# Row maxima turned two or three steps later, their rows written from ScalarE's queue, and one set of three PSUM banks for scores, turn and logits, in a causal attention with routed experts behind it

## The chip, the cores and the metric

One core of a Trainium2 chip. The core has TensorE (PE) for matrix products, VectorE (DVE), ScalarE (ACT), GpSimd (POOL) and SyncE (SP), which only issues transfers. Each engine works through its own list of instructions in order. Here DMA transfers are issued by SP and ACT as well as by POOL; an engine that issues one goes on as soon as the issue is done, unless the instruction itself has to wait for something. The metric is the device time of one execution in microseconds (us). Three executions of the kernel before took 743.34, 747.02 and 748.52 us, median 747.02.

## The reference

Three stages, each feeding the next:

```python
# attention: 4 batches, 8 heads, 576 positions, 64 wide
cum = np.cumsum(np.maximum(s, 0.0), axis=-1)
scores = q @ k.T / 8 + np.minimum(-(cum[i] - cum[j]), 0.0)      # only j <= i, the rest -1e9
attn = np.exp(scores - scores.max(-1)); attn /= attn.sum(-1) + 1e-9
x = attn @ v                                                    # laid out as batch, position, 512
# routed experts: 8 experts, 512 -> 1024 -> 512
logits = x @ w_gate; local = sigmoid(x @ w_local)
e[s] = argmax(logits[s]) if s == 0 or local[s] < 0.5 else e[s-1]
y[s] = softmax(logits[s])[e] * (relu(x[s] @ w1[e]) @ w2[e])
# gated unit: 512 -> 1024 -> 512, a convolution of width 3 along the positions
h = relu(y @ w_in)
out = (h * sigmoid(conv3(h, conv_w))) @ w_out
```

All products have to come out near single precision, so operands are split into a high and a low half-precision part, and a product becomes two or three matrix products.

## The kernel before, in words

**Stages.** Attention runs until about 263 us, then the last logits, the choice of experts and the sorting of tokens (a chain on DVE with short matrix products), then the experts' matrix products from 299 us on, then the gated unit. The change touches only attention and the logits that are made beside it.

**Units and steps.** Attention is cut into eight units, one for four heads of one batch. A unit is 14 steps: for each head the score groups g = 0, 1, 2 and, behind each pair of heads, g = 3 (the last 64 positions of both). `scores` at step t multiplies k by q on PE into a tile z (pool `zps`, three banks of PSUM, L438 and L441). One step later `weights` makes two exponentials of it on ACT, phi in half precision (L475) and p in single (L476). Two steps later `rest` makes the low part plo on DVE (L487). At step 4 behind a pair's last group PE multiplies by v (`values`, L503); normalising and writing out (`norm`, `xout`, `store`, `put`) follow.

**The row maxima.** The exponential needs the maximum of each row of scores, as one more row of k: row 70 of the tiles `K1`, and of `T1` for the tails. It comes from a first, coarser product that is made for a coming unit beside the current one: `stage_a` gives 14 pieces, each some matrix products into a tile za (pool `aps`, two banks, L331) and a reduction on DVE (`mx`, L334). Behind the last piece stand four steps: `max_cols` (DVE, tile m, L397), `max_turn` (PE, one product with the identity that turns the 128x18 columns of maxima into 18 rows, L407, in pool `mps`, one bank), `max_out` (ACT copies the 18 rows into the tile mr, L412) and `max_row` (three transfers: two of eight rows into `K1`, L419, and one of two rows into `T1`, L422). The first `scores` of the unit needs the first of them, and the third `scores` of the unit, at its index 2, the last.

**What sets the order.** Every engine's list is written in program order by a loop over steps t. Work that is not tied to t itself is planned by the table `PAR`: a number says how many steps ahead of a unit's first step t0 the thing is done. `mx` is the step of `max_cols`: -3 for unit 1, -6 for unit 2, -5 for unit 3 and -7 for the units 4 to 7. `max_turn` and `max_out` stand one step behind it, `max_row` two. `at` sets splitting, transposing (`turn`, L256) and copying (L260, L264) of a unit's k and q, `load` and `lv` the loads (L160, L170), `ps` the step at which a finished unit's result is written to memory (`put`, L573, L577). All these transfers are issued by SP (`Q`), in program order; ACT issues only three small ones at the start (L590, L591).

**What a transfer waits for.** Besides the data it needs, each transfer issued by SP or ACT raises one of eight completion counters (DMAHW0 to DMAHW7), which are handed out in turn when the program is built, in the order in which the builder expects the transfers. Before it is issued, its engine waits until the transfer that used that counter last has landed. An engine waiting so does nothing else.

Of the kernel before, what the change touches and what calls it, by code (L numbers as in the profile page):

```python
# [9 lines left out]
F32 = mybir.dt.float32  # L10
# [6 lines left out]
PSUM = bass.MemoryType.PSUM  # L17
# [25 lines left out]
class Keep:  # L43
# [3 lines left out]

PAR = {'u1': {'sv': -6, 'pa': -10, 'pn': 4, 'mx': -3},  # L50
 'u2': {'at': (-24, -23, -20, -20, -19, -16), 'lv': -15, 'sv': -2, 'pa': -14, 'pn': 8, 'mx': -6},
 'u3': {'load': -37, 'loadq': 6, 'at': (-33, -28, -28, -27, -24, -22), 'sv': -1, 'pa': -19, 'pn': 14, 'mx': -5},
 'u': {'load': -48,
       'loadq': 8,
       'at': (-38, -34, -28, -31, -23, -23),
# [1 line left out]
       'sv': -4,  # L57
       'pa': -20,
       'pn': 13,
       'mx': -7},  # L60
 'h': {'rc': 11,
       'lg': 16,
       'co': 1,
# [51 lines left out]
def attention(tc, ctx, q, k, v, s, xd, rt, hook):  # L115
# [8 lines left out]
    V, A, PE, Q, G = nc.vector, nc.scalar, nc.tensor, nc.sync, nc.gpsimd  # L124

    def pool(n, b, on=ctx, **kw):
        return on.enter_context(tc.tile_pool(name=n, bufs=b, **kw))

    const, vp, natv = pool("const", 1), pool("vv", 2), pool("natv", 1)
    pp, p0p, php, wk, xp, xtp = pool("p32", 3), pool("p0", PAR["h"]["p0"]), pool("phl", PAR["h"]["ph"]), pool("wk", 2), pool("xs", 2), pool("xt", 1)  # L130
    zps, aps, ops, mps = (pool(n, b, space=PSUM) for n, b in (("zps", 3), ("aps", 2), ("ops", 2), ("mps", 1)))
    dram = pool("exd", 1, space=bass.MemoryType.DRAM)
    ex, ext = dram.tile([3, 2, B * H, 256], F16, name="ex"), dram.tile([3, B * H, 64], F16, name="ext")
    *big, st2 = hook(-1)
# [16 lines left out]
    T1, T2 = const.tile([71, B, 2, 512], F16, name="t1"), const.tile([128, B, 2, 512], F16, name="t2")  # L151
    U = {}
    src, scale, AT = dict(q=q, k=k), dict(q=QS, k=KS), dict(k=0, q=1)

    def load(u, n):
        b, h0 = u // (H // NH), u % (H // NH) * NH
        t = big[n == "q"][:, 0:1024] if u % 2 == 0 else big[1][:, 1024 + 1024 * AT[n]:2048 + 1024 * AT[n]]
        t = U[u, n] = t.rearrange("p (h c d) -> p h c d", h=NH, c=2)
        for c in range(2):
            Q.dma_start(t[:, :, c], src[n][b, h0:h0 + NH, 256 * c:256 * c + 256].rearrange("h (p t) d -> p h (t d)", t=2))  # L160
# [42 lines left out]
    for tq, tk, n in ((triq, trik, 64), (tailq, tailk, 32)):  # L203
        for r in range(0, 128, n):
            x = dict(compare_op=ALU.is_ge, fill=-2.0 ** 15)
            t, r = r // n % 2, slice(r, r + n)
# [42 lines left out]
    def split_qk(u, n):  # L249
        split_hi(u, n)  # L250
        split_lo(u, n)
# [14 lines left out]
    def split_tail(n):  # L266
        i = AT[n]
        a, h = nt[:, i].rearrange("p h (t d) -> p (h t) d", t=2), ht[:, i]
        A.activation(h[:, :, 1 - i], a, AF.Copy, scale=scale[n])
        V.scalar_tensor_tensor(h[:, :, i], in0=a, scalar=scale[n], in1=h[:, :, 1 - i], op0=ALU.mult, op1=ALU.subtract)  # L270
# [11 lines left out]
    def split_v(u):  # L282
# [10 lines left out]
        for x, dh, dl in ((a, w[:, :, :, 0, 0:64], w[:, :, :, 1, 0:64]), (t, wt[:, :, 0, 0:64], wt[:, :, 1, 0:64])):  # L293
            if u == 0 or not PAR["h"]["vg"]:
                A.activation(dh, x, AF.Copy, scale=VS)
# [89 lines left out]
    def key(hs):  # L385
        return hs.start if hs else 16

    def span(hs, tails):
        return slice(0 if hs else 16, 18 if tails else 8)
# [12 lines left out]
            V.tensor_scalar(m[:, 16:18], mx[:, 16:18], 2.0 ** -12, None, op0=ALU.mult)  # L402

    def max_turn(u, hs=slice(0, 4), tails=True):
        t = U[u, "mt"] = mps.tile([128, 512], F32, name="mt")
        r = span(hs, tails)
        PE.matmul(t[0:r.stop - r.start, 0:128], lhsT=U[u, "16", key(hs)][:, 0:r.stop - r.start] if key(hs) != 16 else U[u, "16", 16][:, 16:18], rhs=id16, start=True, stop=True, skip_group_check=True)  # L407

    def max_out(u, hs=slice(0, 4), tails=True):
        n = span(hs, tails).stop - span(hs, tails).start  # L410
        mr = U[u, "mr", key(hs)] = wk.tile([18, 128], F16, name="mr")
        A.activation(mr[0:n], U[u, "mt"][0:n, 0:128], AF.Copy)  # L412

    def max_row(u, hs=slice(0, 4), tails=True):
        n = 0
        if hs:
            n = 4 * (hs.stop - hs.start)
            for e in range(2):
                Q.dma_start(U[u, 1][70:71, e, 1, 256 * hs.start:256 * hs.stop].rearrange("o (x c) -> o x c", c=128), U[u, "mr", key(hs)][n // 2 * e:n // 2 * e + n // 2])  # L419
        if tails:  # L420
            c = 256 * (u % 2)
            Q.dma_start(T1[70:71, u // 2, 1, c:c + 256].rearrange("o (r c) -> o r c", r=2), U[u, "mr", key(hs)][n:n + 2])  # L422

    st = {}

    def mode(x):

        return PAR["m"][3 * x[1] + x[2]] if x[2] < 3 else "a"

# [121 lines left out]
    def store(u, part):  # L551
# [3 lines left out]
        xh, eng = U[u, "xh"][:, part], G if u < NU - 1 else V  # L555
        if eng is G and PAR["h"]["xg"]:
            G.tensor_copy(xh[:, :, 0], x)
# [41 lines left out]
    def plan(t, f):  # L599
        todo.setdefault(math.floor(t), []).append((t, len(todo), f))  # L600
# [14 lines left out]
    def second_a():  # L615
# [5 lines left out]
        lk1=lambda: load(1, "k"), lq1=lambda: load(1, "q"), st=lambda: (split_tail("k"), split_tail("q")), tt=turn_tail, ct=copy_tail,  # L621
        lv0=lambda: loadv(0, 0, G), lv1=lambda: loadv(0, 1, G if PAR["h"]["vq"] else Q), c1=lambda: constants(G, K1[1]), c2=lambda: (constants(G, K1[2]), tctx.close()),
        pa=begin_a, sk1=lambda: split_qk(1, "k"), sq1=lambda: split_qk(1, "q"), mt0a=lambda: max_turn(0, first, False), mo0a=lambda: max_out(0, first, False),
# [4 lines left out]
        z=lambda: Q.dma_start(xd[NT:NT + 128].rearrange("p (j c) -> p j c", c=256), bc(zero[:, None], [128, 4, 256])))  # L628
    for n, t in PAR["start"].items():
        plan(t, begin_tasks[n])  # L630
# [8 lines left out]
    for u in range(1, NU):  # L639
        t0 = u * PER  # L640
        c = PAR.get(f"u{u}", {}) if u < 4 else PAR.get("u", {})
        if u > 1:
            if u > 2:
                plan(t0 + c["load"], lambda u=u: load(u, "k"))
                plan(t0 + c["load"] + c["loadq"], lambda u=u: load(u, "q"))
            for x, f in zip(c["at"], (lambda u=u: split_qk(u, "k"), lambda u=u: split_qk(u, "q"), lambda u=u: turn(u, 0), lambda u=u: turn(u, 1),
                                 lambda u=u: (extra(u), copy(u, "k")), lambda u=u: copy(u, "q"))):
                plan(t0 + x, f)
        if u % 2 == 0:
            plan(t0 + c["lv"], lambda u=u: loadv(u // 2))  # L650
        plan(t0 + c["sv"], lambda u=u: split_v(u))
        for i in range(14):
            pieces.setdefault(t0 + c["pa"] + i * c["pn"] // 14, []).append((u, i))
        plan(t0 + c["mx"], lambda u=u: max_cols(u))
        plan(t0 + c["mx"] + 1, lambda u=u: max_turn(u))
        plan(t0 + c["mx"] + 1, lambda u=u: max_out(u))
        plan(t0 + c["mx"] + 2, lambda u=u: max_row(u))
    for t in sorted(x for x in todo if x < 0):
        work(t)
    am, P = [], {}  # L660
    for t in range(N + 9):
        if t == N - 2 * PER - 6:
            early.close()
        for f in am:
            f()
        am = []
        work(t)
        at = lambda d: steps[t - d] if 0 <= t - d < N else None
        if at(0):
            scores(at(0))  # L670
        for u, i in pieces.get(t, ()):
            if i == 0:
                P[u] = stage_a(u)
            am.append(P[u][i]())
        if at(1):
            weights(at(1))
        if at(2):
            rest(at(2))
        for d, f in ((4, values), (5, norm), (6, xout)):
            y = at(d)  # L680
            if y and y[2] == (3 if y[1] % 2 else 2):
                f(y[0], y[1])
        y = at(7)
        if y and y[2] == 3 and y != (NU - 1, 1, 3):
            store(y[0], y[1] // 2)
        y = at(8)
        if y and y[1:] == (3, 3):
            u = y[0]
            rt.turn(u, U[u, "xh"], U[u // 2, "xth"] if u % 2 else None, range(2) if u < NU - 1 else range(1, 2))
            if u == NU - 1:  # L690
                put(u, range(1, 2))
        y = at(PAR["h"]["ps"])
        if y and y[1:] == (3, 3) and y[0] < NU - 1:
            put(y[0], range(2))
        if at(9) == (NU - 1, 1, 3):
            store(NU - 1, 0)
            rt.turn(NU - 1, U[NU - 1, "xh"], None, range(1))
            put(NU - 1, range(1))
        y = at(PAR['h']['lg'])
        if y and y[1:] == (3, 3) and y[0] < NU - 1:  # L700
            rt.logits(y[0], mps.tile([128, 512], F32, name="mt"))
        y = at(PAR['h']['lg'] + PAR['h']['co'])
        if y and y[1:] == (3, 3) and y[0] < NU - 1:
            rt.collect(y[0])
        hook(t)
# [751 lines left out]
```

## Time and profile before

| | |
|---|---|
| three runs | 743.34, 747.02, 748.52 us (median 747.02) |
| profiled execution | 745.7 us, span 743.5 us |
| busy share of the span | PE 85%, DVE 62%, ACT 52%, POOL 36% |
| chain that ended last | PE 49%, DMA 6%, DVE 1% of the span; it can be followed back to 310.5 us |
| attention | about 28 to 263 us |
| routing | 264 to 299 us |
| experts | 299 to 545 us |
| gated unit | 550 to 740 us |

The profiled execution is 1.3 us below the median of the three runs and inside their range. A row of a list of work in order of time reads: start, busy time, engine (an ending q means that the engine's sequencer issues a transfer), line, operation, tiles, and in brackets the idle time of the engine before it with what ended it. Neighbouring instructions of one kind are one row, marked x2, x3 and so on.

### The profile page before, as it was taken

The page shows a single profiled execution, that of the slowest core. Times are in us where ns is not written, and L with a number is a line of the kernel's source. Part 1 is how long each engine was busy: PE and PEld are TensorE (multiplying, and loading weights), DVE is VectorE, ACT ScalarE, POOL GpSimd, SP SyncE. Part 2 cuts the span into 40 slices and gives each one's busy share as a digit, 9 for nine tenths or more (in the row PEclk, how much of TensorE's full clock was granted, in tenths as well). Part 3 has the DMA queues.
Part 4 walks back from the last instruction along what each step waited for, and adds up shares of the span by engine and source line. Part 5 has one row for each costly group of instructions (what it writes and reads, how often), then busy time and mean ns, then how long its engine had stood idle before and what let it go on. Part 6 is the DMA issues. An engine that isn't in the chain of part 4 may idle for free.

```text
span 743.5 us, 15702 instructions
## 1 busy us (share of the span) xinstructions
PE 631.6 (85%) x5301; PEld 387.1 (52%) x5301; DVE 464.3 (62%) x838; ACT 383.3 (52%) x640; POOL 265.3 (36%) x367
## 2 busy tenths in 40 slices
PE   0449669988988934779999999999879999999997
PEld 0226547766766832334444444444347776666443
DVE  5527558987979787962587759675108994465000
ACT  4135647666767875543464737352109975455110
POOL 9316757655645247922243443433200000000000
PEclk9999879888989975998999999999989999999999
DMA  9977697878768895399999999966256400000111
GB/s 182 200 138 140 158 165 145 136 165 180 128 142 220 248 265 191 86 220 300 237 281 316 240 295 186 255 146 135 68 97 112 65 1 29 29 15 28 58 43 56
DMA packets 197278, 113.37 MB, mean 152 GB/s; under 512 B 147286, under 2 KB 173182, under 8 KB 197182
## 3 DMA queue, kind: packets, MB, share of 16 engines
q1 hardware_dynamic: 192574, 99.14, 58.5%
q0 software_dynamic: 4272, 12.93, 6.1%
q8 instruction: 48, 0.79, 0.4%
q14 instruction: 48, 0.39, 0.2%
q10 hardware_dynamic: 336, 0.11, 0.1%
HBM read 62.20 MB, written 15.31 MB: 104 GB/s over the span
## 4 chain that ended last, share of the span: by engine, by line
PE 49%; DMA 6%; DVE 1%; issue 0%; ACT 0%; another core or an unknown queue 0%; ACTq 0%; SPq 0%; DVEq 0%
PE hp L1270 13%; PE o L1318 13%; PE hp L1078 12%; PE yp L1078 11%; DMA yd<-ys,idx 4%; DMA ht<-hs 2%; PE xp L1108 1%; DVE r L1034 1%; DMA yt<-yd 0%; DVE hs L1124 0%; ACT xt L1109 0%; DVE ys L1138 0%; ACT ys L1137 0%; ACT s L1321 0%
## 5 line engine op out<-in xcount | busy, mean ns | idle before, releaser
L1078 PE MATMUL hp<-r,xt 128*128 x504 | 114.9, 385 | 8.4 <-ACT xt L1109 5.9
L1078 PE MATMUL yp<-r,ht 128*128 x504 | 112.2, 379 | 1.7 <-PEq L1186 1.1
L1270 PE MATMUL hp<-yt,wi 128*128 128x288 f16 x768 | 97.1, 289 | 2.9 <-DMA yt<-yd 2.9
L334 DVE TENSOR_REDUCE mx<-za 128x1 f32<-128x512 f32 (+4 forms) x113 | 67.7, 612 | 50.1 <-PE za L331 49.6
L1318 PE MATMUL o<-wo,g 128*128 128x512 f16 x432 | 94.5, 379 | 0.0
L487 DVE TENSOR_TENSOR plo<-p,phi 128x512 f16<-128x512 f32 (+1 forms) x104 | 85.1, 819 | 6.4 <-ACT p L476 6.2
L1270 PEld LDWEIGHTS <-wi 128*128 128x128 f16 x768 | 75.8, 99 | 24.5 <-DMA yt<-yd 3.4
L1078 PEld LDWEIGHTS <-xt 128*128 128x128 f16 x504 | 49.9, 99 | 69.5 <-ACT xt L1109 9.1
L475 ACT ACTIVATE phi<-z,lnes 128x512 f16<-128x512 f32 (+1 forms) x104 | 65.5, 629 | 39.3 <-PE z L441 39.2
L1078 PEld LDWEIGHTS <-ht 128*128 128x128 f16 x504 | 48.5, 98 | 57.4 <-issue 1.8
L331 PE MATMUL za<-k 70*128 70x256 f16 (+2 forms) x160 | 40.4, 338 | 41.3 <-DMA k<-k 33.6
L1034 DVE SCALAR_TENSOR_TENSOR r<-st,r 128x512 f32 (+3 forms) x76 | 69.3, 980 | 8.1 <-ACT r L1023 4.7
L438 PE MATMUL z<-k 71*128 71x256 f16 (+2 forms) x320 | 60.5, 311 | 12.3 <-ACT phi L475 6.7
L1139 POOL DMA_INDIRECT yd<-ys,idx x21 | 21.6, 1028 | 135.6 <-DVEq L1062 84.3
L1318 PEld LDWEIGHTS <-g 128*128 128x128 f16 x432 | 42.3, 98 | 49.5
L476 ACT ACTIVATE p<-z,lnes 128x512 f32<-128x512 f32 (+1 forms) x104 | 65.6, 631 | 1.2 <-DVE plo L487 1.1
L1023 ACT ACTIVATE r<-st 128x512 f32 (+3 forms) x84 | 57.0, 760 | 15.4 <-SPq L1071 12.5
L503 PEld LDWEIGHTS <-phi 128*128 128x128 f16 (+2 forms) x896 | 53.4, 108 | 4.8 <-issue 1.0
L503 PE MATMUL o<-vv,phi 128*128 128x65 f16 (+1 forms) x832 | 54.3, 203 | 0.0
L438 PEld LDWEIGHTS <-k 71*128 71x128 f16 x576 | 39.7, 106 | 22.7 <-issue 10.9
L503 PE MATMUL o<-vv,plo 128*128 128x65 f16 (+1 forms) x416 | 51.2, 200 | 0.0
L1287 DVE SCALAR_TENSOR_TENSOR c<-hb,cw,c 128x576 f32<-128x576 f32 x32 | 26.1, 816 | 36.7 <-ACT c L1281 36.7
(255 smaller groups left out, 1018.6 us busy)
## 6 DMA issues: line engine op xcount, KB each, us to landing
st<-in_moe_w_dram SPq DMA_DIRECT2D x8, 2048.0 KB
st<-in_moe_w_dram SPq DMA_DIRECT2D x24, 512.0 KB
out_dram<-s SPq DMA_DIRECT2D x18, 256.0 KB
st<-in_k_dram SPq DMA_DIRECT2D x16, 256.0 KB
st<-in_q_dram SPq DMA_DIRECT2D x16, 256.0 KB
k<-k SPq DMA_DIRECT2D x16, 256.0 KB
xd<-xh SPq DMA_DIRECT2D x16, 256.0 KB
k<-in_moe_w_dram SPq DMA_DIRECT2D x8, 512.0 KB
```

Source lines behind the costliest of these rows:

```text
L331: PE.matmul(out, lhsT=l, rhs=r, start=start, stop=stop, skip_group_check=True)
L334: return lambda: V.tensor_reduce(out, z.rearrange("p (e c) -> p e c", e=m), axis=AX.X, op=ALU.max)
L438: PE.matmul(out, lhsT=ks[i], rhs=qs[i], start=first and not i, stop=False, skip_group_check=True)
L475: A.activation(hi[:, 0:n], z[:, 0:n], AF.Exp, bias=lnes, scale=1.0 / SC)
L476: A.activation(p[:, 0:n], z[:, 0:n], AF.Exp, bias=lnes, scale=1.0 / SC)
L487: (V if md == "a" else G).tensor_tensor(lo[:, 0:n], p[:, 0:n], hi[:, 0:n], op=ALU.subtract)
L503: PE.matmul(out, lhsT=w, rhs=x, start=first, stop=last, skip_group_check=True)
L1023: i = self.nc.scalar.activation(hi, src, AF.Copy, scale=self.scale[w])
L1034: i = nc.vector.scalar_tensor_tensor(lo, in0=src, scalar=sc, in1=hi, op0=ALU.mult, op1=ALU.subtract)
L1078: i = self.nc.tensor.matmul(out, lhsT=lhsT, rhs=self.rings[w][:, c, k, bass.ds(s, 1), f], **kw)
L1270: PE.matmul(st[x][:, n, 0:HN], lhsT=wi[:, c, k, m], rhs=t[:, n, a + k], start=k + a + c == 0, stop=k == 3 and a == 4)
L1318: PE.matmul(o, lhsT=g[:, a, k, 128 * i:128 * i + 128], rhs=wo[:, c, k], start=j == 0, stop=j == 23)
```

## The change

The table gets an entry `mt`, the number of steps from `max_cols` to `max_turn`: 1 for unit 1, 2 for the units 2 and 3, 3 for the units 4 to 7. `max_out` and `max_row` now stand together, one step behind `max_turn` (in the same step for unit 1), and `max_row` is issued by ACT (`A`) instead of SP, but for unit 0. The pool `mps` is gone: the turn and the logits take their bank from `aps`, which has three.

```diff
-PAR = {'u1': {'sv': -6, 'pa': -10, 'pn': 4, 'mx': -3},
- 'u2': {... 'pa': -14, 'pn': 8, 'mx': -6},
- 'u3': {... 'pa': -19, 'pn': 14, 'mx': -5},
+PAR = {'u1': {'sv': -6, 'pa': -10, 'pn': 4, 'mx': -3, 'mt': 1},
+ 'u2': {... 'pa': -14, 'pn': 8, 'mx': -6, 'mt': 2},
+ 'u3': {... 'pa': -19, 'pn': 14, 'mx': -5, 'mt': 2},
  'u': {...
-       'mx': -7},
+       'mx': -7,
+       'mt': 3},
...
-    zps, aps, ops, mps = (pool(n, b, space=PSUM) for n, b in (("zps", 3), ("aps", 2), ("ops", 2), ("mps", 1)))
+    zps, aps, ops = (pool(n, b, space=PSUM) for n, b in (("zps", 3), ("aps", 3), ("ops", 2)))
...
-        t = U[u, "mt"] = mps.tile([128, 512], F32, name="mt")
+        t = U[u, "mt"] = aps.tile([128, 512], F32, name="za")
...
-    def max_row(u, hs=slice(0, 4), tails=True):
+    def max_row(u, hs=slice(0, 4), tails=True, on=Q):
...
-                Q.dma_start(U[u, 1][70:71, e, 1, ...
+                on.dma_start(U[u, 1][70:71, e, 1, ...
...
-            Q.dma_start(T1[70:71, u // 2, 1, c:c + 256]...
+            on.dma_start(T1[70:71, u // 2, 1, c:c + 256]...
...
-        plan(t0 + c["mx"] + 1, lambda u=u: max_turn(u))
-        plan(t0 + c["mx"] + 1, lambda u=u: max_out(u))
-        plan(t0 + c["mx"] + 2, lambda u=u: max_row(u))
+        plan(t0 + c["mx"] + c["mt"], lambda u=u: max_turn(u))
+        plan(t0 + c["mx"] + c["mt"] + (u > 1), lambda u=u: (max_out(u), max_row(u, on=A)))
...
-            rt.logits(y[0], mps.tile([128, 512], F32, name="mt"))
+            rt.logits(y[0], aps.tile([128, 512], F32, name="za"))
```

From line 61 to about line 654 the changed file's numbers are one higher. Three places of the lists show what moves.

The first is PE at the turn of unit 5's maxima, in the steps of unit 4 (L407 is the turn, L438 and L441 the scores of unit 4, L331 a piece of unit 6's maxima). Before it stands ahead of the second score group of the third head:

```order
L438 LDWEIGHTS k_1392
L438 MATMUL z<-k_1392 128x512
L441 LDWEIGHTS identm
L441 MATMUL z<-trik,identm 128x128
L407 LDWEIGHTS m_2926
L407 MATMUL mt<-id_134,m_2926 18x128
L438 LDWEIGHTS k_142
L438 MATMUL z<-k_142 128x128
```

In the changed kernel it stands two steps further on, behind a piece of unit 6's and ahead of the first score group of the fourth head:

```order
L442 LDWEIGHTS identm
L442 MATMUL z<-trik,identm 128x128
L332 LDWEIGHTS k_138
L332 MATMUL za<-k_138 128x256
L332 LDWEIGHTS k_138
L332 MATMUL za<-k_138 128x256
L332 LDWEIGHTS identm
L332 MATMUL za<-triq,identm 128x128
L332 LDWEIGHTS identm
L332 MATMUL za<-triq,identm 128x128
L408 LDWEIGHTS m_2923
L408 MATMUL za<-id_131,m_2923 18x128
```

So two more steps of scores and pieces stand between the making of the maxima and their turn.

The second is ACT at the same unit, with the semaphores that each row waits for. Before, its list has only the copy there, and its transfers are SP's:

```order
L475 ACTIVATE phi<-z,lnes 128x64
L476 ACTIVATE p<-z,lnes 128x64
L412 ACTIVATE mr<-mt 18x128
L238 ACTIVATE st_114<-st_115 128x16x64
L471 ACTIVATE p_2978<-z,lnes 128x512
L475 ACTIVATE phi<-z,lnes 128x512
```

Now the copy and the three transfers stand behind two more pairs of exponentials, and ahead of the pair of unit 4's index 10:

```order
L477 ACTIVATE p<-z,lnes 128x512 [waits DVE_49]
L413 ACTIVATE mr<-za 18x128 [waits DMAHW7_49,PE_49]
L420 DMA k_140<-mr 1x8x128 [waits DMAHW1_49,Activation_49]
L420 DMA k_140<-mr 1x8x128 [waits DMAHW4_49]
L423 DMA t_141<-mr 1x2x128 [waits DMAHW0_49]
L476 ACTIVATE phi<-z,lnes 128x512 [waits PE_49]
L477 ACTIVATE p<-z,lnes 128x512 [waits DVE_49]
```

The transfer of `T1`'s rows now waits on ACT for counter 0.

The third is SP in that stretch: the transposes of unit 3's result (L824, L827), those of unit 7's q (L256), and unit 3's `put` (L573). Before:

```order
L824 DMA_TRANSPOSE xT<-xh 128x16x128 [waits DMAHW4_49,Pool_49]
L827 DMA_TRANSPOSE xTt<-xth 128x4x128 [waits DMAHW5_49,Pool_49]
L419 DMA k_143<-mr 1x8x128 [waits DMAHW6_49,Activation_49]
L419 DMA k_143<-mr 1x8x128 [waits DMAHW7_49]
L422 DMA t_144<-mr 1x2x128 [waits DMAHW0_49]
L256 DMA_TRANSPOSE k_3101<-st_114 128x32x64 [waits PE_49,DMAHW1_49,Activation_49,Pool_49]
L256 DMA_TRANSPOSE k_3101<-st_114 128x32x64 [waits DMAHW2_49]
L573 DMA xd<-xh 128x4x256 [waits DMAHW3_49]
```

Changed:

```order
L824 DMA_TRANSPOSE xT<-xh 128x16x128 [waits DMAHW4_49,Pool_49]
L827 DMA_TRANSPOSE xTt<-xth 128x4x128 [waits DMAHW5_49,Pool_49]
L257 DMA_TRANSPOSE k_3098<-st_111 128x32x64 [waits PE_49,DMAHW6_49,Activation_49,Pool_49]
L257 DMA_TRANSPOSE k_3098<-st_111 128x32x64 [waits DMAHW7_49]
L574 DMA xd<-xh 128x4x256 [waits DMAHW0_49]
L574 DMA xd<-xh 128x4x256 [waits DMAHW2_49]
```

The three rows are gone from SP, and counter 0 is now used by the first half of unit 3's `put`, just ahead of the transfer on ACT that waits for counter 0 (the value it waits for is that `put`'s).

## Rows read from the trace of the kernel before

**Rows 1.** Busy time by engine in two stretches; TensorE's granted clock, DMA share, GB/s.

```profile
core 0: us, PE busy (x) PEld busy (x) DVE busy (x) ACT busy (x) POOL busy (x), PEclk, DMA share, GB/s
...
130.00:159.00 29.00, 24.35 (x362) 19.23 (x360) 26.94 (x63) 17.77 (x34) 17.16 (x20) 0.82 0.79 147
...
187.00:211.00 24.00, 20.88 (x360) 17.13 (x359) 23.62 (x58) 17.37 (x33) 13.46 (x21) 0.98 0.70 129
```

**Rows 2.** PE in order of time: its waits around the maxima, and the experts' start.

```profile
107.76 0.59 PE L331 MATMUL za<-k 70*128 70x128 f16 x4 [5.22 <-DMA k<-k]
...
154.47 0.25 PE L331 MATMUL za<-t 70*64 70x64 f16 x4 [1.82 <-DVE mx L334]
...
158.04 0.28 PE L407 MATMUL mt<-id,m 128*18 128x128 f16 x1 [1.16 <-DVE m L397]
...
171.60 0.61 PE L438 MATMUL z<-k 71*128 71x512 f16 x2 [2.30 <-DMA k<-mr]
...
186.54 0.22 PE L407 MATMUL mt<-id,m 128*18 128x128 f16 x1 [1.85 <-DVE m L397]
...
193.79 0.26 PE L438 MATMUL z<-t 71*64 71x64 f16 x4
...
210.14 0.28 PE L407 MATMUL mt<-id,m 128*18 128x128 f16 x1 [1.74 <-DVE m L397]
...
236.16 0.22 PE L407 MATMUL mt<-id,m 128*18 128x128 f16 x1 [2.05 <-DVE m L397]
...
298.84 5.34 PE L1078 MATMUL hp<-r,xt 128*128 x24 [1.26 <-ACT xt L1109]
```

**Rows 3.** DVE in order of time, behind the turns of units 4 and 6.

```profile
160.38 1.33 DVE L334 TENSOR_REDUCE mx<-za 128x4 f32<-128x512 f32 x2 [1.00 <-PE za L331]
...
213.11 1.33 DVE L334 TENSOR_REDUCE mx<-za 128x4 f32<-128x512 f32 x2 [1.63 <-PE za L331]
```

**Rows 4.** SP in order of time: transfers issued late.

```profile
8.56 8.24 SPq L256 DMA_TRANSPOSE k<-h  x4
...
102.18 1.39 SPq L264 DMA_DIRECT2D k<-k  x2
...
138.17 8.04 SPq L256 DMA_TRANSPOSE k<-st  x2
...
167.96 1.51 SPq L419 DMA_DIRECT2D k<-mr  x2
...
192.29 7.10 SPq L256 DMA_TRANSPOSE k<-st  x2
199.44 1.84 SPq L573 DMA_DIRECT2D xd<-xh  x2
```

**Rows 5.** ACT in order of time: its own transfers, unit 4's copy, unit 5's, idle places.

```profile
13.89 0.46 ACTq L591 DMA_DIRECT2D ext<-cp  x1
...
158.35 0.27 ACT L412 ACTIVATE mr<-mt 18x128 f16<-18x128 f32 x1 [1.93 <-PE mt L407]
...
166.30 0.69 ACT L475 ACTIVATE phi<-z,lnes 128x512 f16<-128x512 f32 x1 [1.90 <-PE z L441]
...
186.80 0.27 ACT L412 ACTIVATE mr<-mt 18x128 f16<-18x128 f32 x1 [1.69 <-PE mt L407]
...
190.77 0.66 ACT L475 ACTIVATE phi<-z,lnes 128x512 f16<-128x512 f32 x1
...
242.62 0.69 ACT L475 ACTIVATE phi<-z,lnes 128x512 f16<-128x512 f32 x1 [1.95 <-PE z L441]
```

**Rows 6.** POOL in order of time: the low part of unit 7's q.

```profile
189.23 2.12 POOL L247 TENSOR_TENSOR st<-st,st 128x1024 f16<-128x1024 f32 x1
```

**Rows 7.** Single lines: number, duration in ns (least, median, most), first and last start.

```profile
L419 SPq DMA_DIRECT2D k<-mr x18: 585/692/994, 34.2 to 240.2; - x18
...
L422 SPq DMA_DIRECT2D t<-mr x8: 589/598/619, 48.9 to 240.9; - x8
...
L256 SPq DMA_TRANSPOSE k<-st x8: 3075/3770/4744, 38.8 to 195.4; - x8
```

More of the change, by code (lines that the diff above doesn't have):

```diff
@@ L44 @@
     pass
-PAR = {'u1': {'sv': -6, 'pa': -10, 'pn': 4, 'mx': -3},
- 'u2': {'at': (-24, -23, -20, -20, -19, -16), 'lv': -15, 'sv': -2, 'pa': -14, 'pn': 8, 'mx': -6},
- 'u3': {'load': -37, 'loadq': 6, 'at': (-33, -28, -28, -27, -24, -22), 'sv': -1, 'pa': -19, 'pn': 14, 'mx': -5},
+PAR = {'u1': {'sv': -6, 'pa': -10, 'pn': 4, 'mx': -3, 'mt': 1},
+ 'u2': {'at': (-24, -23, -20, -20, -19, -16), 'lv': -15, 'sv': -2, 'pa': -14, 'pn': 8, 'mx': -6, 'mt': 2},
+ 'u3': {'load': -37, 'loadq': 6, 'at': (-33, -28, -28, -27, -24, -22), 'sv': -1, 'pa': -19, 'pn': 14, 'mx': -5, 'mt': 2},
  'u': {'load': -48,
@@ L418, in max_row @@
             for e in range(2):
-                Q.dma_start(U[u, 1][70:71, e, 1, 256 * hs.start:256 * hs.stop].rearrange("o (x c) -> o x c", c=128), U[u, "mr", key(hs)][n // 2 * e:n // 2 * e + n // 2])
+                on.dma_start(U[u, 1][70:71, e, 1, 256 * hs.start:256 * hs.stop].rearrange("o (x c) -> o x c", c=128), U[u, "mr", key(hs)][n // 2 * e:n // 2 * e + n // 2])
         if tails:
             c = 256 * (u % 2)
-            Q.dma_start(T1[70:71, u // 2, 1, c:c + 256].rearrange("o (r c) -> o r c", r=2), U[u, "mr", key(hs)][n:n + 2])
+            on.dma_start(T1[70:71, u // 2, 1, c:c + 256].rearrange("o (r c) -> o r c", r=2), U[u, "mr", key(hs)][n:n + 2])
     st = {}
```

## The prediction, as made before the changed kernel ran

> **What bounds the kernel now.** I read the chain of waits first. It can be followed back only to 310.5 us, where it lies in the experts' products, but these begin at 298.84 behind the routing [rows 2], and the routing is one serial chain of short DVE and PE instructions that begins with the last unit's result. So I take a microsecond won or lost in attention as a microsecond at the end, one for one. Next I looked at attention's stretches by engine. In 130 to 159 us DVE is busy 26.94 of 29 us and PE 24.35; in 187 to 211 us DVE 23.62 of 24 and PE 20.88; ACT has 17.77 of 29 and 17.37 of 24 [rows 1]. DVE is the tight engine there, and ACT has about a third of its time free. Then I read PE's list for its waits [rows 2]: 5.22 us for a copy of k, 1.82 for a maximum on DVE, 2.30 for the maxima rows of unit 4, and 1.16, 1.85, 1.74 and 2.05 at the turns of units 4 to 7, where PE stands until `max_cols` is done. Last I read SP's list, because the 2.30 is no matter of data: unit 4's rows lay ready at 158.62 (the copy's 158.35 + 0.27 [rows 5]), and SP issued them at 167.96 [rows 4], 9.3 us later, because other transfers stood ahead.
>
> The sum is made against the profiled execution, 745.7 us; the median of the runs, 747.02, is 1.3 above it.
>
> **Gains, place by place.**
>
> The turns of units 4 to 7 come two steps later (a step is about 2 us: 14 of them lie in some 28 us). All four waits are under 2.1 us, so they go whole at their place; the question is what they hide. Behind the turns of units 4 and 6 DVE sits idle for 1.00 and 1.63 us, waiting for the piece that PE makes next [rows 3]: there the wait of PE became a wait of the tight engine. I take the two waits whole, 1.2 and 1.7 (bounds 0 and that). Behind the turn of unit 5 DVE has no hole; it is busy in all but 0.4 us of the 24 [rows 1], so PE catches up and waits for DVE instead: 0 (at most 1.85). At unit 7 PE has little of its own to wait for otherwise, and ACT shows a hole of 1.95 behind [rows 5]; I take half of the 2.05: 1.0 (0 to 2.05).
>
> Unit 4's rows on ACT: the copy is issued two pairs of exponentials later than now, at about 163, three issues behind it take under 2 us (0.692, 0.692 and 0.598 on SP [rows 7]), and landing takes 2.1 (issue ended 167.96 + 1.51 = 169.47, PE freed at 171.60 [rows 2, 4]). That is 167, ahead of the 169.3 at which PE came. The 2.30 goes (0 to 2.3); next late there would be DVE's reductions.
>
> SP gets 2.0 us shorter per unit (the same three issues). Its list is without holes where the copy of k for the 5.22 us wait is issued at 102.18 [rows 4], and unit 1's rows stand ahead of it, so that copy comes up to 2.0 earlier: 2.0 (0 to 2.0).
>
> The third bank for za lets PE run one piece further ahead of DVE. It can only save where PE waits for a reduction, as in the 1.82 at 154.47; DVE stays the bound there: 0.5 (0 to 1.8). While a turn or logits hold one of the three banks, two are left, which is what za has now, so I set no loss against it.
>
> The gains are 1.2 + 1.7 + 0 + 1.0 + 2.3 + 2.0 + 0.5 = 8.7; all upper ends together make 12.9.
>
> **Losses.**
>
> ACT's own work: three issues for each of seven units. On ACT an issue took 0.46 once, on SP 0.59 to 0.99 [rows 5, 7], so 1.4 to 2.0 per unit, 10 to 14 in all. ACT waits for z for 1.90 and 1.95 us at such places [rows 5] and has a third of its time free, so a pair of exponentials that comes 1.5 later still comes before PE runs out of banks for z (three). I take 0.5 (0 to 4, two units uncovered).
>
> The counters. Here a new wait is added to ACT, and behind it on ACT stand all later exponentials. **At unit 5** the transfer of `T1`'s rows waits for counter 0, which unit 3's `put` used last. That `put` stands on SP behind the two transposes of unit 7's q, and these need POOL's low part, which ends at 191.35 (189.23 + 2.12 [rows 6]). Before, they were issued from 192.29 for 7.10 us and the `put` followed at 199.44 [rows 4]. With SP's own three rows gone they can begin at 191.4 at the earliest, or at 189.7 if ACT's share of the split is not held by the 1.69 us wait for the turn any more [rows 5]; the first half of the `put` is then issued by 197.7 to 199.4 and lands 2.1 later, at 199.8 to 201.5. ACT comes to the waiting transfer where unit 4's pair of index 10 begins now, 190.77 [rows 5], plus about 1 for the two issues ahead. So ACT stands for 8 to 9.5 us. PE can make the z of two or three more steps and has the values of older steps to do; it stops about at index 13, 193.79 [rows 2], until the pair of index 10 is done, about 201. Once freed, ACT catches up at 0.66 per exponential [rows 5]. DVE, the bound, has about 2 us of reductions and subtractions in hand, then waits as well. I price it at what DVE loses, 8 minus 2, so 6; bounds 3 (if half is made up behind) and 9 (nothing in hand). It does not lock up: nothing that the `put` needs stands behind that transfer.
>
> **At unit 3** the same transfer waits for one of SP's transposes for unit 5, issued before from 138.17 for 8.04 both [rows 4]; only the first counts, and it can begin about 2 earlier without SP's rows. ACT would come at about 139.5: hold 0 to 2.5, taken as 0.5, as DVE's list behind covers most. At unit 7 a margin of about half a microsecond is left, at units 1, 2, 4 and 6 the counters' earlier transfers are old: 0.
>
> The losses are 0.5 + 6 + 0.5 = 7.0.
>
> **Sum.** 745.7 - 8.7 + 7.0 = 744.0, and 745.3 when set beside the median: I forecast 745, no change that can be told from none. One per cent is 7.5 us here, about what a measurement of this kernel can tell.
>
> **A rule against the change.** SP's four transposes at the start were in issue from 8.56 to 16.80 [rows 4], and inside that time ACT issued a transfer in 0.46 us at 13.89 [rows 5]: no sign that the one holds up the other. The Trainium skill, "Perfetto Trace Analysis", section "DMA Instruction — HWDGE (DVE, Sync)", says that the block which makes the descriptors is locked for one instruction's exclusive use, and that the next sequencer's lock wait counts in the shown duration; by that, ACT's rows would each wait for a transpose's issue. The row speaks against it, but the rule makes a rival.
>
> **The rivals.**
>
> *No hold (0.25).* If unit 3's `put` lands before ACT comes, or PE, DVE and ACT have more in hand than I think, the 6 does not come. For it: ACT may come later than 191, since the whole of attention moves. Against it: 7.10 us of transposes stand ahead of the `put`. The time: 745.3 - 6 = 739; with the upper ends of two turns and the banks, 736.
>
> *ACT's issue is held by SP's transposes (0.08, slower).* At units 2 to 7 SP has transposes beside the rows; one takes 3.77 us at the median [rows 7]. ACT has about 1.9 free at such a place, so each would cost 1.9, six of them 11: 745.3 + 11 = 756. It decides if ACT's issues take over 1.5 us each. Against it: 0.46 at 13.89.
>
> *A longer hold (0.09, slower).* ACT's wait at unit 5 delays its share of what POOL and SP need next, so that the units behind it find their `put` and transposes late too, unit 7 first, whose margin is half a microsecond. With the hold at 9, unit 3's at 2.5 and a third of 3, and the gains at half (4.3), the time is 747.0 - 4.3 + 14.5 = 757. It decides if ACT's wait at unit 5 is over 10 us or comes at a second unit with over 2.
>
> *My forecast (0.58)*, gains and hold nearly cancel: 740 to 751, by the bounds 3 and 9 of the hold and some 5 up or down in the gains.
>
> **The numbers.** Faster by over 1% (under 739.5) is three quarters of the first rival and a tenth of the forecast: 0.25. Slower by over 1% (over 754.5) is nearly all of the two slow rivals and a tenth of the forecast's upper side: 0.18. The rest, 0.57, is within 1%. The range leaves out the far part of the first rival and of the two slow ones: 737 to 753.
>
> **What would show it.** Right: no wait at the turns of units 4 to 7; no wait for mr's rows at unit 5's beginning (171.60 now); on ACT at about 191 to 200 an idle stretch of 8 us or so in front of L423, ended by `xd<-xh`, with PE waiting behind for ACT's phi and DVE for p; ACT's issues of about 0.5 us each. Wrong: no such stretch (then the first rival), issues of 2 us and more on ACT (then the second), a second hold at units 3 or 7 (then the third), or the PE waits at the turns coming back as waits for DVE's mx in the pieces beside them, in which case the gains were never there and the time is 750.

## The result and the profile after

Four of five executions of the changed kernel took 752.85 to 755.6 us; the median of all five is 754.1. The ratio to the kernel before is 1.0105 (95% interval 1.0063 to 1.0147). It is 1% slower; 745, no change, was forecast, and the range ended at 753. The fifth execution took 1698.08 us, more than twice the others, and is left out of the ratio. The kernel before was run five times in all; its median stays 747.02. The profiled execution took 754.1 us with a span of 751.5, which is 8.0 more than before.

The loss lies in attention: the experts' first product starts at 308.59 where it started at 298.84 [rows 2], 9.75 later. PE's list of the changed kernel in order of time, at the places of [rows 2]:

```profile
104.68 0.58 PE L332 MATMUL za<-k 70*128 70x128 f16 x4 [2.48 <-DMA k<-k]
...
144.17 1.01 PE L439 MATMUL z<-k 71*128 71x512 f16 x2 [4.26 <-DMA k<-mr]
...
164.28 0.27 PE L408 MATMUL za<-id,m 128*18 128x128 f16 x1 [3.64 <-DVE mx L335]
...
188.01 0.58 PE L332 MATMUL za<-k 70*128 70x128 f16 x4 [3.52 <-DVE plo L488]
...
202.65 0.32 PE L439 MATMUL z<-t 71*64 71x64 f16 x4 [5.48 <-ACT p L477]
...
225.49 0.22 PE L408 MATMUL za<-id,m 128*18 128x128 f16 x1 [1.71 <-DVE mx L335]
...
245.05 0.22 PE L408 MATMUL za<-id,m 128*18 128x128 f16 x1 [0.89 <-DVE m L398]
...
308.59 0.59 PE L1078 MATMUL hp<-r,xt 128*128 x2 [1.26 <-ACT xt L1109]
```

The wait for k has gone from 5.22 to 2.48, and that for unit 4's rows is gone. The waits at the turns are gone at unit 5 only: at unit 7 0.89 is left, and at units 4 and 6 they are 3.64 and 1.71, now ended by a reduction of a piece (`mx`, L335) instead of `max_cols`. Three waits are new: 4.26 for unit 3's rows, 3.52 for `plo` at 188.01, and 5.48 for p at 202.65. Behind the last stands ACT, here at unit 5's rows, in order of time:

```profile
191.81 0.25 ACT L413 ACTIVATE mr<-za 18x128 f16<-18x128 f32 x1
192.09 2.27 ACTq L420 DMA_DIRECT2D k<-mr  x2
200.70 0.59 ACTq L423 DMA_DIRECT2D t<-mr  x1
201.34 0.69 ACT L476 ACTIVATE phi<-z,lnes 128x512 f16<-128x512 f32 x1 [9.27 <-DMA xd<-xh]
```

SP beside it:

```profile
190.16 6.21 SPq L257 DMA_TRANSPOSE k<-st  x2
196.41 2.82 SPq L574 DMA_DIRECT2D xd<-xh  x2
```

ACT issues the two `K1` rows by 194.36 and then does nothing until 200.70, which is 6.3 us; the 9.27 counts from the copy `mr` to the next exponential, with the three issues in it. The profile names unit 3's `put` (`xd<-xh`), which SP could issue only at 196.41, behind its two transposes. DVE has nothing to subtract meanwhile:

```profile
202.63 0.69 DVE L488 TENSOR_TENSOR plo<-p,phi 128x512 f16<-128x512 f32 x1 [5.63 <-ACT p L477]
```

### The profile page after: what moved, and what is told of

It reads as the page before. It is cut to its first block, busy times and chain, and to the rows that moved or that the text cites. A ratio compares the mean times of both kernels' runs of the same rounds, so it can differ in the third digit from the quotient of the medians.

```text
span 751.5 us, 15698 instructions
## 1 busy us (share of the span) xinstructions
PE 634.9 (84%) x5301; PEld 393.1 (52%) x5301; DVE 466.9 (62%) x838; ACT 383.2 (51%) x640; POOL 264.2 (35%) x367
## 5 line engine op out<-in xcount | busy, mean ns | idle before, releaser
L1078 PE MATMUL hp<-r,xt 128*128 x504 | 112.2, 379 | 9.4 <-ACT xt L1109 7.9
L488 DVE TENSOR_TENSOR plo<-p,phi 128x512 f16<-128x512 f32 (+1 forms) x104 | 86.9, 837 | 15.9 <-ACT p L477 15.8
L335 DVE TENSOR_REDUCE mx<-za 128x1 f32<-128x512 f32 (+4 forms) x113 | 66.5, 612 | 40.6 <-PE za L332 40.5
L439 PE MATMUL z<-k 71*128 71x256 f16 (+2 forms) x320 | 62.2, 318 | 10.9 <-DMA k<-mr 8.1
L504 PEld LDWEIGHTS <-phi 128*128 128x128 f16 (+2 forms) x896 | 57.7, 114 | 5.4 <-issue 1.3
L504 PE MATMUL o<-vv,phi 128*128 128x65 f16 (+1 forms) x832 | 58.2, 209 | 0.0
L504 PE MATMUL o<-vv,plo 128*128 128x65 f16 (+1 forms) x416 | 54.4, 206 | 0.0
```

The source lines that it names most:

```text
L335: return lambda: V.tensor_reduce(out, z.rearrange("p (e c) -> p e c", e=m), axis=AX.X, op=ALU.max)
L439: PE.matmul(out, lhsT=ks[i], rhs=qs[i], start=first and not i, stop=False, skip_group_check=True)
L488: (V if md == "a" else G).tensor_tensor(lo[:, 0:n], p[:, 0:n], hi[:, 0:n], op=ALU.subtract)
L504: PE.matmul(out, lhsT=w, rhs=x, start=first, stop=last, skip_group_check=True)
L1078: i = self.nc.tensor.matmul(out, lhsT=lhsT, rhs=self.rings[w][:, c, k, bass.ds(s, 1), f], **kw)
```

## The experiments

The theory is that this wait of ACT, in front of all later exponentials, is what makes the change slower. The first rival: the time goes with the late turn and the shared banks, and the wait only covers it. Each ratio is to the kernel before on the same chip, with its 95% interval.

**Unit 5's `T1` row by SP.** One transfer of the change is undone.

```diff
-            on.dma_start(T1[70:71, ...
+            (Q if u == 5 else on).dma_start(T1[70:71, ...
```

> The changed kernel, but unit 5's transfer of T1's rows is issued by SP again; its two K1 rows stay on ACT and now wait for counters of transfers that landed long before (a put at 180 us, a copy from ex at 181). If the counter's wait on ACT (9.27 us in front of the exponential at 201.34) is what made the change slower: that stretch vanishes, the fifth unit begins about 8 us earlier, 746 us. If the later turn and the shared banks cost the time and the stretch only covers them: 752 to 754.

0.9991 (0.9953 to 1.0029). ACT at the same place:

```profile
190.68 0.25 ACT L413 ACTIVATE mr<-za 18x128 f16<-18x128 f32 x1
190.96 1.31 ACTq L420 DMA_DIRECT2D k<-mr  x2
192.32 0.69 ACT L476 ACTIVATE phi<-z,lnes 128x512 f16<-128x512 f32 x1 [1.39 <-PE za L332]
```

The stretch is gone, and with it the whole loss.

**Every `put` two steps later.** No row of maxima is moved; the counters fall otherwise, and the writes of the results come later.

```diff
-       'ps': 18},
+       'ps': 20},
```

> The changed kernel with every unit's put two steps later (20 in place of 18), so that the counters fall otherwise: unit 5's three transfers on ACT wait for copies of k and a transpose that landed before 185 us. Same theory as for unit 5's row on SP, without moving a row: if the counter is the cause, 746 us and no stretch on ACT at 192; if rows on ACT in themselves hold ACT, 753.

0.9971 (0.9927 to 1.0016). Three rows by ACT, no wait for a counter:

```profile
186.88 1.31 ACTq L420 DMA_DIRECT2D k<-mr  x2
188.24 0.59 ACTq L423 DMA_DIRECT2D t<-mr  x1
188.88 0.69 ACT L476 ACTIVATE phi<-z,lnes 128x512 f16<-128x512 f32 x1 [2.02 <-DMA k<-mr]
```

The 2.02 is now only the three issues and what lies between them.

**Unit 3's turn one step earlier.**

```diff
- 'u3': {... 'mx': -5, 'mt': 2},
+ 'u3': {... 'mx': -5, 'mt': 1},
```

> The changed kernel with unit 3's turn one step behind its maxima instead of two. PE waits 4.26 us for unit 3's rows at 144.17 although ACT issued them by 138.07. If they are late because they are issued late (two steps behind their old place): that wait falls to under 2.5 and the time by 2 to 3, 751 us. If they are late because transposes of SP fill the transfer engines from 132 to 140: they land at the same time and nothing changes, 754.

1.0152 (1.0102 to 1.0202). PE's wait at unit 3's start is gone, and PE waits 1.35 at that unit's turn instead. But PE now comes to that start later than the rows were there in the changed kernel, 144.17:

```profile
145.26 1.04 PE L439 MATMUL z<-k 71*128 71x512 f16 x2
```

So this run does not tell whether the rows had been late because they were issued late or because they took long to land (issued by 138.07, there at 144.17). The time did not fall. ACT still stood 8.75 us at unit 5.

**Banks as before.** Two for za, one for turn and logits, all else as changed.

```diff
-    zps, aps, ops = (... ("zps", 3), ("aps", 3), ("ops", 2)))
+    zps, aps, ops, mps = (... ("zps", 3), ("aps", 2), ("ops", 2), ("mps", 1)))
```

> The changed kernel with the banks as before (two for za, one for turn and logits); turn and queue as in the changed kernel, and the same counter for unit 5's last row. If the turn waits at 164.28 (3.64 us, ended by a reduction of za) and 225.49 (1.71) because it needs a bank that a piece still holds: both waits vanish and the time falls by 2 to 4, 751. If DVE's backlog sets the pace with either set of banks, the waits move to the pieces and the time stays at 754.

1.0203 (1.0151 to 1.0254). The wait beside unit 4's turn is still there, 3.97, now at the piece ahead of the turn:

```profile
168.20 0.59 PE L332 MATMUL za<-k 70*128 70x256 f16 x2 [3.97 <-DVE mx L335]
```

So a bank of its own for the turn does not take the wait away: it goes over to the piece, which waits for DVE's reductions too. ACT stood at unit 3 for a transpose's counter and at unit 5 for the `put`'s, longer than in the first profile of the changed kernel:

```profile
146.02 0.69 ACT L476 ACTIVATE phi<-z,lnes 128x512 f16<-128x512 f32 x1 [7.82 <-DMA k<-st]
...
206.70 0.69 ACT L476 ACTIVATE phi<-z,lnes 128x512 f16<-128x512 f32 x1 [10.29 <-DMA xd<-xh]
```

Since the waits differ too, this run says nothing on what the banks are worth.

**One part at a time.** The next four put parts of the change into the kernel before. Queue alone (turn and rows at their old places):

```diff
-        plan(t0 + c["mx"] + 2, lambda u=u: max_row(u))
+        plan(t0 + c["mx"] + 2, lambda u=u: max_row(u, on=A))
```

> The kernel before with one part of the change: the maxima rows of units 1 to 7 are issued by ACT, at their old place; turn and banks as before. Their counters were last used by transfers that should have landed (unit 5: a put issued at about 179 us in the kernel before). If SP's shorter list and unit 4's rows are the gain I priced (2.0 + 2.3): no wait for mr's rows at unit 4's start, the experts' first product 4 us earlier, 738 against 742.3 on this chip. If issuing on ACT costs as much as it saves: 742 or more, with ACT standing on counters at units 3 or 7.

0.992 (0.9883 to 0.9956), the lowest ratio of all, though some intervals below overlap it. The experts' first product starts at 292.86, 5.98 ahead of the kernel before. Unit 4 starts without a wait; PE still waits at every turn:

```profile
157.98 0.28 PE L408 MATMUL mt<-id,m 128*18 128x128 f16 x1 [1.42 <-DVE m L398]
...
169.21 0.60 PE L439 MATMUL z<-k 71*128 71x512 f16 x2
...
183.98 0.23 PE L408 MATMUL mt<-id,m 128*18 128x128 f16 x1 [2.17 <-DVE m L398]
...
207.57 0.23 PE L408 MATMUL mt<-id,m 128*18 128x128 f16 x1 [1.74 <-DVE m L398]
...
230.40 0.22 PE L408 MATMUL mt<-id,m 128*18 128x128 f16 x1 [2.06 <-DVE m L398]
```

Turn alone (`mt` as in the change, rows by SP, banks as before):

```diff
+        plan(t0 + c["mx"] + c["mt"], lambda u=u: max_turn(u))
+        plan(t0 + c["mx"] + c["mt"] + (u > 1), lambda u=u: (max_out(u), max_row(u, on=Q)))
```

> The kernel before with the later turn alone; rows by SP, banks as before. My sum's term for the turns (1.2 + 1.7 + 1.0) would give 738, less what later rows cost on SP's full list (unit 4's wait of 2.30 grows by up to 4): 738 to 742. The rival: DVE's reductions set the pace there, the waits at the turns only move to the pieces beside them, and the later rows cost 4: 746.

1.0029 (1.0001 to 1.0056), as the rival expected. PE's waits at the turns of units 4 to 6 are gone, and these stand in their place:

```profile
190.14 0.58 PE L332 MATMUL za<-k 70*128 70x128 f16 x4 [5.91 <-DMA k<-k]
...
216.47 0.38 PE L332 MATMUL za<-k 70*128 70x128 f16 x4 [2.39 <-DMA k<-k]
...
228.97 0.63 PE L439 MATMUL z<-k 71*128 71x512 f16 x2 [3.61 <-DMA k<-mr]
```

SP waits for the later `mr`, and all behind it with it: unit 7's transposes begin at 196.46, before at 192.29 [rows 4].

```profile
194.22 1.48 SPq L420 DMA_DIRECT2D k<-mr  x2
195.74 0.60 SPq L423 DMA_DIRECT2D t<-mr  x1
196.46 7.31 SPq L257 DMA_TRANSPOSE k<-st  x2
```

In this one profile the experts begin at 307.52, 8.68 later than before, while the ratio of the runs is worth only some 2 us; why the two differ is open.

Banks alone (pool `aps` with three, `mps` gone):

> The kernel before with the three shared banks alone. By my sum 0.5 faster: 742. By the comparison of the split banks in the changed kernel (1.0203 against 1.0105) sharing is worth some 7 us when turn and rows come late; if it is worth that by itself: 736 to 738.

1.0007 (0.9973 to 1.0041): nothing. The 1.82 of [rows 2] ahead of unit 4's turn is gone, and the wait at the turn has grown from 1.16 to 3.36:

```profile
157.60 0.22 PE L408 MATMUL za<-id,m 128*18 128x128 f16 x1 [3.36 <-DVE m L398]
```

With one more bank PE gets further ahead and then waits longer for the same engine.

Turn and banks, rows by SP (the changed kernel with `on=Q`):

> The changed kernel with the rows issued by SP again, turn late and banks shared. If the queue is the whole of the loss (the counter on ACT): faster than the kernel before by the turns and banks, 738 to 740. If rows that come two steps later are too late on SP's list: PE waits for mr's rows at the starts of units 3 to 6 for 2 to 6 us each, 748 or more, and the change of queue is needed with the later turn.

1.002 (0.9988 to 1.0051). PE waits for rows at the starts of units 1 and 6 (7.96 and 3.10) and for copies of k at 108.46, 158.59 and 188.10 (7.08, 3.81, 5.66); neither half of the expectation was right, the late rows cost about as much as the turns gave.

**Queue and banks, turn at its old place.**

> The changed kernel with the turn, the copy and the rows at their old places: queue and banks of the change without its later turn. If the later turn is what brings the put's counter onto ACT: no stretch of 8 us on ACT at unit 5, and the time of the queue alone, 0.992 of before. If rows on ACT and shared banks hurt each other by themselves (a turn that needs a bank of za and holds it until ACT comes): 1.00 or more.

0.9957 (0.9919 to 0.9996), an interval that overlaps the queue alone's. At unit 5 ACT has no wait for a counter: between the rows and the next exponential lie 0.79 us. The late turn is what brought them together with the `put`.

**Late turn by ACT without the wait, banks as before** (`ps` 20).

> Rows on ACT and the later turn with the banks as before, and put at 20, so that unit 5 waits for no late counter (unit 3's last row still waits for the counter of a transpose for unit 5). If the later turn is worth something once the wait for the put is gone: 0.990 or less. If it only moves PE's waits to the pieces, because DVE sets the pace: 0.992 to 1.000, and a wait of 2 to 6 at unit 3's start.

0.9958 (0.9916 to 0.9999): an interval that overlaps the queue alone's, and not the 0.990 at which the turn would have shown a worth of its own.

**One step only.** `mt` 1 for units 1 to 3 and 2 for the rest, copy and rows in the turn's step, `ps` 20.

> A version to beat both: rows on ACT together with the copy, the turn one step later for units 4 to 7 only, shared banks, put at 20; all of unit 5's counters last used by copies and a transpose that landed before. If one step is enough to take PE's waits at the turns (1.2 to 2.1 each) and they count: 0.985. If DVE sets the pace: the same as the queue alone, 0.992.

1.0006 (0.9959 to 1.0053). Neither half of the expectation was right: it is not 0.985, and it lies above the queue alone's whole interval. Why is open.

**The changed kernel again.**

> The changed kernel once more, for what a second profiled execution repeats. Attention: the experts' first product within 1.5 us of the first profile's 308.6, ACT's stretch at unit 5 of 8 to 10 us again. The experts: if the waits of 2 to 3 us with a lower granted clock behind them belong to single executions, they stand in other places or are gone, and the experts take 3 to 6 us more or less; if they belong to the kernel, they stand at 340 and 462 again. Ratio to before 1.006 to 1.015.

1.0188 (1.0125 to 1.0252). The ratio, the start of the experts' first product (311.20) and ACT's stretch are all above what was expected; ACT stood at unit 3 also:

```profile
143.76 0.69 ACT L476 ACTIVATE phi<-z,lnes 128x512 f16<-128x512 f32 x1 [5.62 <-DMA k<-mr]
...
208.01 0.69 ACT L476 ACTIVATE phi<-z,lnes 128x512 f16<-128x512 f32 x1 [12.01 <-DMA xd<-xh]
```

Unit 3's row by `T1` was issued at 143.12, 3.5 behind the first two; the first profile had 0.5 there. So the kernel's waits differ from execution to execution, and its ratio was 1.0105 in one set of runs and 1.0188 in another.

**The length of the wait changed.** The two removals also changed other counters. Here unit 3's `put` alone is planned otherwise, to stand between SP's two transposes, and in a second run ahead of both; ACT's transfers still wait for counters of that `put`.

```diff
-        if y and y[1:] == (3, 3) and y[0] < NU - 1:
+        if y and y[1:] == (3, 3) and y[0] < NU - 1 and y[0] != 3:
             put(y[0], range(2))
+        y = at(13)            # 10 in the second
+        if y and y == (3, 3, 3):
+            put(3, range(2))
```

> The changed kernel with only unit 3's put planned earlier (13 steps in place of 18): on SP it now stands between the two transposes of unit 7's q instead of behind them. Unit 5's transfers on ACT still wait for that put's counters. If the length of ACT's wait is what costs the time, one transpose less (3 to 4 us) stands ahead: a stretch of 5 to 8 us where there were 9.3 and 12.0, the time 3 to 5 us under the changed kernel, ratio about 1.005 to 1.010. If having to wait at all, or what the rows on ACT push back, costs it: 1.010 to 1.019 as before.

> The same with unit 3's put ahead of both transposes (10 steps): the rows on ACT still wait for counters of that put and of a transpose of its tails. By the length of the wait: a stretch of 0 to 4 us, ratio 0.995 to 1.002, as in the two runs without that wait. By the rival: 1.010 or more.

1.0123 (1.0073 to 1.0174) and 1.003 (0.9989 to 1.0072). ACT, in the first and then in the second:

```profile
193.79 5.82 ACTq L420 DMA_DIRECT2D k<-mr  x2
199.64 0.59 ACTq L423 DMA_DIRECT2D t<-mr  x1
200.28 0.69 ACT L476 ACTIVATE phi<-z,lnes 128x512 f16<-128x512 f32 x1 [6.53 <-DMA k<-mr]
```

```profile
195.23 2.96 ACTq L420 DMA_DIRECT2D k<-mr  x2
198.23 0.59 ACTq L423 DMA_DIRECT2D t<-mr  x1
198.88 0.69 ACT L476 ACTIVATE phi<-z,lnes 128x512 f16<-128x512 f32 x1 [4.88 <-DMA k<-mr]
```

The second came out nearly as the theory says, stretch and ratio both a little above what was expected. In the first the stretch shrank as expected, but its time cannot be told from the changed kernel's and lies where the rival had it; its profile has, ahead of unit 5, a wait of 5.30 for a copy of k that the changed kernel has shorter (3.52, for DVE). What the wait itself does is seen at its own place, from PE's first scores of unit 4's fourth head to those of unit 5's third head. ACT's stretch is the time before its next exponential, with the issues of some 2 us in it:

| kernel | ACT's stretch at unit 5, us | from head to head, us |
|---|---|---|
| before | none | 207.75 - 189.00 = 18.75 |
| queue alone | 0.83 | 205.18 - 186.44 = 18.74 |
| row of unit 5 by SP | 1.39 | 208.58 - 190.27 = 18.31 |
| put later | 2.02 | 204.01 - 186.19 = 17.82 |
| put ahead of both transposes | 4.88 | 212.28 - 193.63 = 18.65 |
| put ahead of one | 6.53 | 217.95 - 193.09 = 24.86 |
| unit 3's turn early | 8.75 | 223.34 - 195.35 = 27.99 |
| changed | 9.27 | 220.91 - 191.40 = 29.51 |
| banks as before | 10.29 | 226.12 - 195.75 = 30.37 |
| changed, again | 12.01 | 224.34 - 195.63 = 28.71 |

Up to 4.9 us cost nothing, 6.5 and more cost 6 to 12. Each row is one profile.

## Why the prediction was wrong

**The wait on ACT: mechanism right, size of its cost wrong.** The place (L423 at unit 5), the cause (unit 3's `put` behind two transposes, by way of counter 0) and the end (199.8 to 201.5; ACT went on at 200.70) came as forecast. ACT came to the waiting transfer later than forecast, at 194.36 where 191 or 192 was expected, so that it stood there for 6.3 us and not for 8 to 9.5. The failed step is the price: "what DVE loses, 8 minus 2, so 6", with bounds 3 and 9. From head to head the stretch took 10.8 more than before, and 11.2 more than with only that row back on SP: more than the upper bound, for a wait shorter than forecast. By the ratios of the two removals against the changed kernel's first (1.0105 less 0.9991 and 0.9971) it is 1.1 to 1.3%, 8.5 to 10 us, though these were taken in different sets of runs. Two things stand in the place of the 6. DVE did wait 5.63 us (its row at 202.63), near the forecast; but a part of the price comes behind it: PE's granted clock in the changed kernel, by stretches:

```profile
core 0: us, PE busy (x) PEld busy (x) DVE busy (x) ACT busy (x) POOL busy (x), PEclk, DMA share, GB/s
...
192.00:197.00 5.00, 5.00 (x91) 4.40 (x88) 4.37 (x6) 0.06 (x1) 4.64 (x6) 0.87 1.06 116
197.00:202.00 5.00, 0.17 (x3) 0.11 (x1) 0.01 (x1) 0.67 (x2) 0.00 (x0) 0.81 0.89 196
202.00:207.00 5.00, 4.35 (x36) 3.69 (x36) 3.69 (x9) 3.85 (x9) 1.48 (x1) 0.50 0.42 87
207.00:212.00 5.00, 5.00 (x62) 3.99 (x61) 3.55 (x14) 2.60 (x5) 0.00 (x0) 0.50 0.88 206
212.00:217.00 5.00, 5.00 (x59) 3.82 (x58) 2.98 (x7) 2.47 (x4) 0.00 (x0) 0.50 0.33 73
217.00:222.00 5.00, 5.00 (x88) 3.96 (x87) 3.64 (x10) 3.66 (x8) 0.64 (x1) 0.98 0.01 3
```

For some 15 us behind the wait PE had half its clock, 1.2 GHz, where it had 0.98 over 187 to 211 before [rows 1]; from 207 on it is busy throughout at that pace, so PE, not DVE, sets it. I had counted the wait and not the slow stretch that follows it. An estimate from these rows: over 202 to 217 DVE was busy for 10.2 of the 15 us, so with DVE setting the pace the slow clock cost at most 4.8 there, about what the price was short by (10.8 less 6). That the clock is the whole of the difference is read from these rows, not tried.

**The gains: most of the 8.7 did not come.** By the sum attention was to end 1.7 earlier (8.7 less 7.0); it ended 9.75 later. Of these 11.5 the wait's price makes up 4.8; the other 6.7 are gains that were missing and smaller losses, and how they divide is open. The changed kernel was 2.4 behind even before the wait (191.40 against 189.00 in the table). The queue's part was there: 2.0 + 2.3 less 0.5 were priced, and the queue alone brought 0.8% (0.4 to 1.2), 3 to 9 us. The turns' part (1.2 + 1.7 + 1.0) failed. DVE sets the pace there, as the prediction said of unit 5 and, under what would show it wrong, of all: the waits came back as waits for `mx` in the pieces or in the turn. The prediction gave 750 for that ending; with the 4.8 it is 755. By itself the late turn was 1.0029; by its rows, what PE no longer waits for at the turn SP then waits for, with transposes and copies behind it. The hole of DVE behind a turn, on which the two terms rested [rows 3], showed that DVE waits there for PE once; it did not show that the time is lost, since the late turn by ACT without the wait was no faster than the queue alone, which kept all four waits. The banks' 0.5 cannot be told from 1.0007.

**Unit 3** was priced at 0.5, at most 2.5. In the first profile its rows came late for PE by 4.26 us, which I had not thought of: moved one step on from their old place, they are issued by 138.07, PE needs them at 139.9, and they are there at 144.17, 6.1 behind the issue, where the forecast took 2.1 for a landing. In others ACT stood there too, up to 5.62 in the repeat and 7.82 with the banks as before. With unit 3's turn early the time stayed, so what that costs is open.

**ACT's issues** took 0.59 to 0.65 each in most places, as forecast, and apart from the waits above their 2 us per unit bring a wait that is new in PE's list only behind unit 7's, 1.05 for p at 250.46. The slowest of the 14 `K1` rows took 1.58, beside a transpose. The rival by which a transpose's issue holds ACT's is out: the changed kernel's issue of unit 5's rows began at 192.09, inside SP's transposes of 190.16 to 196.37, and the two were done by 194.36. The rule of the Trainium skill, "Perfetto Trace Analysis", section "DMA Instruction — HWDGE (DVE, Sync)", that the descriptor block is locked for one instruction at a time, may be in that 1.58; it is no more here.

**The third rival** (a longer hold, or a second one) is what the repeat showed: stretches of 12.01 at unit 5 and 5.62 at unit 3. It had 0.09; the prediction took one length for a wait that differs by 3 us between executions of one kernel, so that the first profile's end of the wait fell within the forecast is in part luck.

## What to carry to other kernels

When transfers move to another engine's queue, look up for each what its completion counter was used for last: a counter ties an engine with work behind it to a transfer on a queue that has nothing to do with it, and a step more or less in the order decides whether that transfer is old or still to be issued. Price such a wait as its whole length beyond what is in hand, and what follows it at the lower clock too. A wait of PE for the engine that sets the pace is no gain by itself; try the queue's part by itself first, since here it alone was worth 0.8%.

## What the runs showed of the hardware

The experts' part, which the change does not touch, differs by 5 us and more between executions: from the first block's product to the twenty-first's it took 206.0 us in the queue alone's profile, 211.1 in that of the kernel before and 215.3 with the later put. With the later put the experts began 5.16 ahead of the kernel before (293.68 against 298.84), but only 0.94 were left sixteen blocks later. This wait lies between, PE in order of time and then the granted clock:

```profile
452.20 8.11 PE L1078 MATMUL hp<-r,xt 128*128 x24 [3.40 <-ACT xt L1109]
```

```profile
446.00:452.00 6.00, 2.80 (x13) 1.07 (x11) 4.90 (x6) 5.03 (x9) 4.05 (x4) 0.92 1.00 180
452.00:458.00 6.00, 5.80 (x15) 2.13 (x16) 5.86 (x12) 5.88 (x13) 1.98 (x3) 0.51 0.90 219
```

In most blocks these 24 products take 5.34 [rows 2]; behind the wait they took 8.11 at a granted clock of 0.51. The kernel before has such a wait too, 3.34 ahead of its fifth block's 8.08. The changed kernel waited 2.14 at its block there in one profile, 0.85 in the other. So for one profiled execution the start of the experts' first product says more of attention than the whole time does. It is no proof by itself: with the late turn alone it came 8.68 later, and the runs took hardly longer (1.0029).
